# Retention attention feeding a GELU MLP: a hand-ordered two-stream schedule with groups of 256 to 768 tokens and loads by chunk

## Chip, cores, metric

One core of a Trainium2 chip. The time is the device time of one execution in microseconds (us), the median of several. Executions of one kernel agree within about 1% here, apart from one of the kernel before at 354.67 us, which is left out. Engines: PE is TensorE, DVE VectorE, ACT ScalarE, Pool GpSimd. Lines such as L66 are source lines of the kernel at hand.

## The reference, cut

```python
# q, k, v: [4 batches, 8 heads, 768 tokens, 64]; lam: [8]; w_in: [512, 2048]; w_out: [2048, 512]
intra = (qb @ kb.T * Dmask) @ vb                 # Dmask[i, j] = lam ** (i - j) for i >= j
inter = (qb * lam ** (pos + 1)) @ kv_state       # the state runs over the blocks of a sequence
kv_state = lam ** block * kv_state + (kb * lam ** (block - 1 - pos)).T @ vb
x = attention, [3072 tokens, 512]
out = gelu(x @ w_in) @ w_out                     # exact gelu
```

Both kernels work in bf16 with chunks of 128 tokens, 24 in all, 6 to a batch. They scale rows by lam^pos and lam^-pos, so that the mask is plainly triangular.

## The kernel before

The parts that matter (cuts marked). Its tool orders the instructions; the source order is only the dataflow.

```python
TOK = 256
def attn_batch(b, psum):
    # one load per tensor and batch, [128, H, NB, D]
    nc.gpsimd.dma_start(q_t, q[b].rearrange("h (so si) d -> si h so d", si=128))    # k_t, v_t alike
    for sb in range(NB):                                                  # 6 chunks
        nc.gpsimd.tensor_mul(q_hat, q_t[:, :, sb, :], lam_pos_b)
        nc.gpsimd.tensor_mul(k_hat, k_t[:, :, sb, :], lam_neg_b)
        # ... 8 transposes on PE, two copies on DVE, 8 score matmuls on PE
        nc.vector.tensor_mul(sc_m, sc_ps, cmask_b)
        # ... 16 output matmuls, a copy to xT_sb on ACT; 8 matmuls k_hat.T v,
        # ... two state additions and one state multiplication on DVE
def moe_chunk(t, psum_m, psum_mo):
    for kf in range(NK2):                                                 # 16 feature blocks
        # ... 4 matmuls of N=256 into h_ps (two buffers)
        nc.scalar.activation(gT, h_ps, ACT.Gelu)
        for io in range(NO):                                              # 2 token tiles
            nc.tensor.matmul(om[io], gT[:, io * 128:(io + 1) * 128], w_out_t[:, kf, :], ...)   # N=512
for b in range(B):
    attn_batch(b, psum)
    # ... after batch 0: one load each of w_in and w_out
    for t in range(b * (S // TOK), (b + 1) * (S // TOK)):
        moe_chunk(t, moe_psum, moe_out_psum)
```

## Time and profile before

| | before |
|---|---|
| median of the three fast runs | 297.76 us (297.51 to 298.76; 298.26 with the slow one) |
| profiled span | 296.9 us |
| PE busy, with overlapping latencies | 238.1 us |
| DVE, ACT, Pool busy | 85.6, 103.8, 94.7 us |
| MLP's own matmuls at their warm spacing | 167 us |

### The profile page before, as it was taken

The page shows a single profiled execution, that of the slowest core. Times are in us where ns is not written, and L with a number is a line of the kernel's source. Part 1 is how long each engine was busy: PE and PEld are TensorE (multiplying, and loading weights), DVE is VectorE, ACT ScalarE, POOL GpSimd, SP SyncE. Part 2 cuts the span into 40 slices and gives each one's busy share as a digit, 9 for nine tenths or more (in the row PEclk, how much of TensorE's full clock was granted, in tenths as well). Part 3 has the DMA queues.
Part 4 walks back from the last instruction along what each step waited for, and adds up shares of the span by engine and source line. Part 5 has one row for each costly group of instructions (what it writes and reads, how often), then busy time and mean ns, then how long its engine had stood idle before and what let it go on. Part 6 is the DMA issues. An engine that isn't in the chain of part 4 may idle for free.

```text
span 296.9 us, 5123 instructions
## 1 busy us (share of the span) xinstructions
PE 238.1 (80%) x2081; PEld 145.1 (49%) x2112; DVE 85.6 (29%) x150; ACT 103.8 (35%) x247; POOL 94.7 (32%) x119
## 2 busy tenths in 40 slices
PE   0037295999999789999999799999998789999893
PEld 0025162555555456655554555555555556555451
DVE  1037544400000679500000768300003778100000
ACT  4001221343344323353534223453533133453532
POOL 7474625847200778610000645300003531000000
PEclk9999997999999969999999879999999689999999
DMA  6996999999990194990010100010101000010101
GB/s 44 157 118 116 187 192 126 123 146 137 154 174 0 71 80 30 106 152 27 6 68 0 73 0 2 2 71 0 73 1 56 17 2 1 2 71 2 71 1 71
DMA packets 80135, 20.25 MB, mean 68 GB/s; under 512 B 74480, under 2 KB 76528, under 8 KB 80112
## 3 DMA queue, kind: packets, MB, share of 16 engines
q0 software_dynamic: 76512, 13.63, 67.0%
q1 hardware_dynamic: 3600, 6.30, 5.6%
q8 instruction: 16, 0.26, 0.4%
q14 instruction: 7, 0.06, 0.1%
HBM read 27.27 MB, written 6.29 MB: 113 GB/s over the span
## 4 chain that ended last, share of the span: by engine, by line
PE 60%; ACT 12%; DMA 9%; issue 7%; DVE 6%; POOL 4%; ACTq 1%; POOLq 0%
PE omps L167 32%; PE h_ps L162 16%; ACT gT L165 11%; DMA w_out_t<-in_moe_w_out_dram 5%; DMA k_t<-in_k_dram 4%; PE sc_ps L124 3%; PE out_ps L135 3%; DVE sc_m L130 3%; PE out_ps L136 2%; PE kT_ps L113 2%; POOL q_hat L104 1%; DVE kv_state_new L153 1%; PE qT_ps L112 1%; POOL k_hat L105 1%; PE kv_ps L143 1%
## 5 line engine op out<-in xcount | busy, mean ns | idle before, releaser
L162 PE MATMUL h_ps<-xT_sb,w_in_t 128*128 128x256 bf16 x768 | 116.4, 279 | 4.0 <-DMA w_in_t<-in_moe_w_in_dram 4.0
L167 PE MATMUL omps<-w_out_t,gT 128*128 128x512 bf16 x353 | 105.3, 386 | 15.8 <-ACT gT L165 4.4
L165 ACT ACTIVATE gT<-h_ps 128x256 bf16<-128x256 f32 x192 | 73.1, 384 | 127.2 <-PE h_ps L162 117.2
L162 PEld LDWEIGHTS <-w_in_t 128*128 128x128 bf16 x768 | 76.0, 100 | 42.1 <-DMA w_in_t<-in_moe_w_in_dram 4.3
L167 PEld LDWEIGHTS <-gT 128*128 128x128 bf16 x384 | 29.6, 98 | 50.6 <-ACT gT L165 35.9
L104 POOL TENSOR_TENSOR q_hat<-q_t,lam_pos 128x512 bf16<-128x512 bf16 x24 | 25.1, 1052 | 78.3 <-PE qT_ps L112 57.7
L116 DVE COPY qT<-qT_ps 128x512 bf16<-128x512 bf16 x24 | 10.1, 421 | 122.5 <-PE qT_ps L112 119.8
L130 DVE TENSOR_TENSOR sc_m<-sc_ps,cmask 128x1024 bf16<-128x1024 f32 x24 | 29.4, 1224 | 28.8 <-PE sc_ps L124 28.7
L105 POOL TENSOR_TENSOR k_hat<-k_t,lam_neg 128x512 bf16<-128x512 bf16 x24 | 25.7, 1071 | 34.5 <-PE kv_ps L143 26.9
L138 ACT CAST xT_sb<-out_ps 128x512 bf16<-128x512 f32 x24 | 14.0, 585 | 55.4 <-PE out_ps L136 55.4
L112 PE MATMUL qT_ps<-ident,q_hat 128*128 128x128 bf16 x96 | 12.3, 251 | 17.2 <-POOL q_hat L104 17.1
L135 PE MATMUL out_ps<-sc_m,v_t 128*64 128x128 bf16 x192 | 16.5, 248 | 7.2 <-DVE sc_m L130 6.0
L153 DVE TENSOR_TENSOR kv_state_new<-kv_state_new,lam_blk 128x512 bf16<-128x512 bf16 x24 | 18.0, 749 | 1.8
L112 PEld LDWEIGHTS <-q_hat 128*128 128x128 bf16 x96 | 7.9, 111 | 19.8 <-POOL q_hat L104 17.6
L124 PE MATMUL sc_ps<-qT,kT 64*128 64x128 bf16 x192 | 11.4, 247 | 5.7 <-DVE kT L117 5.4
L149 POOL MEMSET kv_state_new<- 64x256 bf16 x24 | 7.3, 306 | 27.0 <-PE out_ps L136 26.3
L135 PEld LDWEIGHTS <-v_t 128*64 128x64 bf16 x192 | 12.9, 125 | 5.7 <-issue 5.3
L113 PE MATMUL kT_ps<-ident,k_hat 128*128 128x128 bf16 x96 | 11.8, 245 | 3.6 <-POOL k_hat L105 2.5
L171 ACT COPY out_sb<-omps 128x512 f32<-128x512 f32 x24 | 12.9, 589 | 4.8 <-PE omps L167 4.6
L136 PE MATMUL out_ps<-qT,kv_state_new 128*64 128x128 bf16 x160 | 13.6, 245 | 0.0
L117 DVE COPY kT<-kT_ps 128x512 bf16<-128x512 bf16 x24 | 10.1, 420 | 11.0 <-PE kT_ps L113 10.6
L96 POOL DMA_DIRECT2D v_t<-in_v_dram x4 | 8.9, 2225 | 12.8 <-DMA q_t<-in_q_dram 6.0
(35 smaller groups left out, 100.1 us busy)
## 6 DMA issues: line engine op xcount, KB each, us to landing
out_dram<-out_sb SPq DMA_DIRECT2D x24, 256.0 KB, 2.2
q_t<-in_q_dram POOLq DMA_DIRECT2D x4, 768.0 KB, 9.5
k_t<-in_k_dram POOLq DMA_DIRECT2D x4, 768.0 KB, 11.6
v_t<-in_v_dram POOLq DMA_DIRECT2D x4, 768.0 KB, 10.8
w_in_t<-in_moe_w_in_dram POOLq DMA_DIRECT2D x1, 2048.0 KB, 13.5
w_out_t<-in_moe_w_out_dram POOLq DMA_DIRECT2D x1, 2048.0 KB, 15.1
lam_b<-in_lam_dram SPq DMA_DIRECT2D x1, 4.0 KB, 2.5
```

The source lines that it names most:

```text
L104: nc.gpsimd.tensor_mul(q_hat, q_t[:, :, sb, :], lam_pos_b)
L105: nc.gpsimd.tensor_mul(k_hat, k_t[:, :, sb, :], lam_neg_b)
L112: nc.tensor.transpose(qT_ps[:, hp * C:(hp + 1) * C], q_hat[:, 2 * hp:2 * hp + 2, :], ident)
L113: nc.tensor.transpose(kT_ps[:, hp * C:(hp + 1) * C], k_hat[:, 2 * hp:2 * hp + 2, :], ident)
L124: nc.tensor.matmul(sc_ps[:, (hi * HP + hp) * C:(hi * HP + hp + 1) * C], kT[hi * D:(hi + 1) * D, hp * C:(hp + 1) * C], qT[hi * D:(hi + 1) * ...
L130: nc.vector.tensor_mul(sc_m, sc_ps.rearrange("p (h c) -> p h c", h=H), cmask_b)
L135: nc.tensor.matmul(osl, vb[:, h, :], sc_m[:, hi * HP + hp, :], start=True, stop=False)
L136: nc.tensor.matmul(osl, kv_state[:, h * D:(h + 1) * D], qT[:, hp * C:(hp + 1) * C], start=False, stop=True)
L153: nc.vector.tensor_mul(kv_state_new, kv_state_new, lam_blk_hd)
L162: nc.tensor.matmul(h_ps, w_in_t[:, ki, kf * 128:(kf + 1) * 128], x_t[:, ki, :], start=(ki == 0), stop=(ki == NK1 - 1))
L165: nc.scalar.activation(gT, h_ps, ACT.Gelu)
L167: nc.tensor.matmul(om[io], gT[:, io * 128:(io + 1) * 128], w_out_t[:, kf, :], start=(kf == 0), stop=(kf == NK2 - 1))
```

## The change

Its intent is to keep PE on MLP matmuls and to slip the pieces of the next group's attention between them at fixed places, so that neither the gelu nor the attention's chain is waited for. The diff is 409 lines; this is its core.

```diff
-    TOK = 256
+    groups = [6, 2, 4, 4, 4, 4]                 # chunks of 128 tokens in a group
+    ctx.enter_context(tc.manual_schedule())     # every engine runs in source order
+    def load_piece(b, name, lo, hi):            # one load per tensor and chunk, [128, NB, H, D]
+        for so in range(lo, hi):
+            nc.gpsimd.dma_start(qkv[b, name][:, so, :, :],
+                src[b, :, so * C:(so + 1) * C, :].rearrange("h si d -> si h d"))
+    # batch 0: chunks 0 and 1, constants, chunks 2 to 5, then w_in and w_out in 4 slices each
+    def hats(n):                                # Pool; k is no longer scaled, v is
+        nc.gpsimd.tensor_mul(c.q_hat, ..., lam_pos_b)
+        nc.gpsimd.tensor_mul(c.v_hat, ..., lam_neg_b)
+    # transposes: one copy of q and k on DVE; scores: mask and state additions on DVE,
+    # state multiplication on Pool; outputs: state product as 4 full 128x128 matmuls, copy on DVE
+    # mlp_blocks: first all of mm1 (4 matmuls, gelu), then mm2 (4 matmuls a block)
+    live[0] = hats(0)                           # lead-in: group 0 alone
+    for n in range(groups[0]):
+        transposes(live[n])
+        if n + 1 < groups[0]: live[n + 1] = hats(n + 1)
+        scores(live[n]); outputs(live[n], xT[0], n)
+    load_batch(1)                               # 18 loads
+    for g in range(len(groups)):
+        first = 0.45 if g == 0 else 0.0
+        at = lambda f: (first + (0.97 - first) * (i + f) / m) * total
+        def step(kind):
+            if kind == 0:
+                if n % NB == 0 and n // NB + 1 < B: load_batch(n // NB + 1)
+                live[n] = hats(n)
+            # ... 1 transposes, 2 scores, 3 outputs
+        todo += [(at(-0.3), 0, step), (at(0.05), 1, step), (at(0.4), 2, step), (at(0.75), 3, step)]
+        # ... MLP blocks in order, each step issued once its place is reached
```

## The prediction

> **What bounds the kernel now.** I read first the page's busy times and slices, then the windows by stage, then the steady part of the timeline, then the Pool engine's own timeline at the start.
>
> ```profile
> span 296.9 us, 5123 instructions
> PE 238.1 (80%) x2081; PEld 145.1 (49%) x2112; DVE 85.6 (29%) x150; ACT 103.8 (35%) x247; POOL 94.7 (32%) x119
> PEclk9999997999999969999999879999999689999999
> ```
>
> PE (TensorE) carries the time; nothing else is above 35%. But 238.1 us counts overlapping matmul latencies, so it is no measure of what PE needs. The third line is the clock by slice: after the first batch it dips three more times, at the starts of batches 1 to 3.
>
> The windows of three stages: MLP alone, the start of batch 1, the start.
>
> ```profile
> core 0: us, PE busy (x) PEld busy (x) DVE busy (x) ACT busy (x) POOL busy (x), PEclk, DMA share, GB/s
> 0.00:37.00 37.00, 9.65 (x112) 6.43 (x112) 12.72 (x24) 6.05 (x9) 22.19 (x30) 1.00 1.73 124
> ...
> 98.00:107.00 9.00, 6.17 (x92) 4.38 (x90) 7.67 (x15) 2.24 (x4) 7.87 (x8) 0.77 0.16 60
> ...
> 190.00:228.00 38.00, 35.50 (x230) 20.81 (x232) 0.61 (x2) 16.48 (x42) 0.56 (x1) 1.00 0.08 29
> ```
>
> So there are three losses. At the start PE has little to do for 37 us. At a batch start (98 to 107) the attention chain of 128-token chunks runs nearly alone, with DVE busy 7.67 of 9 us and PE's clock at 0.77. And inside the MLP PE waits for the gelu. That last one is in the timeline of the steady part:
>
> ```profile
> 87.03 0.82 ACT L165 ACTIVATE gT<-h_ps 128x256 bf16<-128x256 f32 x2 [1.19 <-PE h_ps L162]
> 87.47 0.11 PEld L167 LDWEIGHTS <-gT 128*128 128x128 bf16 x2 [0.38 <-ACT gT L165]
> ...
> 89.05 0.82 ACT L165 ACTIVATE gT<-h_ps 128x256 bf16<-128x256 f32 x2 [1.19 <-PE h_ps L162]
> 89.48 0.11 PEld L167 LDWEIGHTS <-gT 128*128 128x128 bf16 x2 [0.38 <-ACT gT L165]
> ```
>
> Two feature blocks repeat every 2.01 us. From the same view, seven N=256 matmuls take 0.93 us with 0.27 of latency, so they start (0.93 - 0.27)/6 = 0.11 us apart; four N=512 ones take 1.04 with 0.38, so 0.22 apart. The work of two blocks is 8 x 0.109 + 4 x 0.217 = 1.74 us. So 0.27 us in 2.01, 13%, is waiting. Over 96 such pairs that is 26 us.
>
> PE's floor is then: MLP 768 x 0.109 + 384 x 0.217 = 167 us, plus attention. The remaining 100 us are what a better order could save.
>
> Pool at the start is the view on which my prediction turns:
>
> ```profile
> 1.82 2.39 POOL L94 DMA_DIRECT2D q_t<-in_q_dram  x1
> 4.21 2.22 POOL L95 DMA_DIRECT2D k_t<-in_k_dram  x1
> 11.85 2.22 POOL L96 DMA_DIRECT2D v_t<-in_v_dram  x1 [5.42 <-DMA q_t<-in_q_dram]
> 14.08 1.05 POOL L104 TENSOR_TENSOR q_hat<-q_t,lam_pos 128x512 bf16<-128x512 bf16 x1
> ...
> 23.54 0.81 POOL L180 DMA_DIRECT2D w_in_t<-in_moe_w_in_dram  x1
> ...
> 33.42 1.22 POOL L181 DMA_DIRECT2D w_out_t<-in_moe_w_out_dram  x1
> ```
>
> A load occupies Pool while it is issued, and the multiplication behind it starts only then (14.08 follows 11.85 + 2.22). By the source, a batch load moves 6144 rows of 64 numbers, w_in 512 long rows, w_out 2048. A line through 0.81, 1.22 and about 2.25 us is 0.68 us plus 0.26 us per 1000 rows.
>
> **The Trainium skill.** "TensorE: Matmul & The Clock Gate", Wait — 56ns, not 53.3ns?, gives a warm spacing of N/2.4 GHz plus 2.5 ns: 109 and 216 ns at N = 256 and 512. The trace agrees. The same page, What's actually happening, says that the clock halves after about 3.4 us of idle and returns after as much work; the dips agree, and in the first chunks the trace shows the N=128 transposes at twice their later spacing. "DMA: Bandwidth & Descriptors", Anatomy of one DMA, calls descriptor generation small and says many come before the cost shows up; here it is 0.81 to 2.39 us of Pool per load, and the measurement decides. "Perfetto Trace Analysis", DMA Instruction — SWDGE (GPSIMD), says the reported end of such an instruction is the end of descriptor generation; the trace agrees, as Pool's next work begins there.
>
> **The change part by part.**
>
> *Loads by chunk.* 12 loads become 72 of 1024 rows. Each costs 0.68 + 0.27 = 0.95 us of Pool (estimate from the line above); a batch goes from 6.7 to 17.1 us of Pool. Eight weight slices of 512 rows cost 0.81 each, 6.5 us. Data lands as fast as before (a tensor of a batch about every 5.2 us), so the landing is no limit. But the new order is fixed: all 18 loads of batch 0 and all 8 weight slices stand in front of the first multiplication. Pool is free at about 0.8 + 17.1 + 1.1 (constants) + 6.5 = 25.5 us. The first multiplication was at 14.08 before.
>
> *Six attention chunks alone.* DVE per chunk, scaled from the rows of the page (0.42 for 512 bf16 out of PSUM, 1.22 for 1024 f32, 0.42 for 256 f32, so 0.155 us plus elements at 1 or 2 per 0.96 GHz cycle): one joint copy of q and k transposed 0.69, mask 1.22, two state additions 0.84, and the copy of the result, moved from ACT, 0.69; 3.44 in all. The wait for the scores between copy and mask is 0.65, handoffs 0.2. That is 4.3 us a chunk, and Pool's 3.2 (two multiplications of 1.05, two half-size ones estimated at 0.55) fits below. First transposes at 26.5, copy at 27.5, six chunks: the MLP starts at about 53 us. The weights have landed by then (some 27 us after about 20).
>
> *512-token groups.* The first matmuls are N=384, 256 and 512. Sum of the MLP: 128 x 0.163 + 64 x 0.109 + 256 x 0.216 + 384 x 0.216 = 166 us, as before. The second matmuls now come after all 16 gelus, so the wait of 0.27 per pair goes. What remains is the double-buffered PSUM tile: four matmuls, 0.1 us, then the gelu (0.384 us at 256; about 0.59 at 512, as the equal-sized ACT copies take 0.585). A pair of N=512 blocks needs 1.78 us against 1.73 of work, N=384 1.47 against 1.30, N=256 1.14 against 0.87: 16 x 0.05/2 x 4 + 32 x 0.085 + 16 x 0.13, so 6 us, of which I keep 5 since attention pieces fill some.
>
> *Attention between the matmuls.* From warm stretches of the timeline: transposes 0.44, scores 0.33, state product 0.25, outputs about 0.22 + 0.3. That is 1.5 us per chunk, 27 us for 18, now without the chain's waits or cold clock.
>
> *Loads ahead of use.* The load of a batch is issued just ahead of the first multiplication of the batch before it. Batches 1 and 2 go out back to back after the lead-in: Pool is free at about 49.5, and 34 us later, at 83.6, multiplies chunk 6. PE meets chunk 6's transposes at fraction 0.463 of the first group, at 53 + 1.7 (cold) + 30 blocks x 0.735, some 77 us. It waits about 7.5 us. Batch 3 is loaded after chunk 11's multiplication, some 3 us before group 1 ends, 17 us of Pool, plus 1 us for the multiplication, while PE wants chunk 12 one block into group 2. It waits about 14.5 us. Each wait exceeds 3.4 us, so some 1.7 us more at half clock.
>
> Sum: start 53, MLP 166, attention 27, gelu 5, cold start 2, Pool waits 22, cold after them 3.5, short handoffs 3, and the end as now 4.5 (last matmul 292.4 to 296.9). 286 us.
>
> **The rivals.** (a) *Pool is not in the way.* If the issue of small loads overlaps more than I reckon (0.5 us each), the start shortens by 8, the first wait goes and the second halves: about 262. For it: a hand-tuned order should not have been left with such waits, and the fraction 0.45 for the first group looks tuned. Against it: three row counts lie on one line, and the fixed 0.68 is paid for each. (b) *The order on PE binds.* PE is in order, so pieces that come too early stall it. In group 1 four chunks share 14 us of MLP: 1.2 us of matmuls lie between scores and outputs, and mask and latencies take 1.6. If every chunk lost 1 us so, 18 us would come on top: about 300. Against it: in the four-chunk groups 2 to 4 there are 2.4 us between pieces. (c) *Vector becomes the bound.* 24 x 3.4 = 82 us in 286; no. (d) *The long lead-in gives back all of the gain*, as it is 4 us longer than the 49 us at which the MLP gets going now. It can't undo it: the waits of 26 us and the three batch starts are gone whatever the start costs.
>
> **Range and chances.** The sum is 286. My largest term is Pool's 0.95 us: 0.1 us less gives 7 us. The likelier error is that I overrate Pool's waits, so I put the time a little under the sum, at 282, and the range at 264 to 294. Below 291.8 counts as faster by over 2%: 0.83; within 2% 0.14; slower 0.03.
>
> **What would show it.** Right: Pool at work on loads without a break up to about 25 us and the first transposes just after; 4.3 us per chunk in the lead-in; the first gelu at 53 to 55; two PE waits for a multiplication on Pool, of some 7 and 14 us, each with the clock down after it; between them N=512 matmuls every 0.216 us. Wrong: first transposes before 20 us, or no such waits (then 255 to 265), or many waits of PE for the mask in each group (then about 300).

## More of the kernel before

The span is far longer than what the matmuls need back to back; the question is which waits make up the rest. The prediction shows the lines of the page, the windows and the timelines for that. One more, the chain of waits that ended last, by engine:

```profile
PE 60%; ACT 12%; DMA 9%; issue 7%; DVE 6%; POOL 4%; ACTq 1%; POOLq 0%
```

Pool is 4% of that chain.

## The result

The changed kernel took 285.61 us (284.87 to 287.21, four runs). The ratio of fast runs is 0.959, 95% interval 0.955 to 0.964. Ratios are the mean time of one kernel's fast runs over that of the other's of the same rounds, so not quite the ratio of the medians quoted. It is 4% faster; the range held, and the sum of 286 us was nearer than the 282 put down.

The page of the changed kernel, its head, its clock by slice and its chain by engine:

```profile
span 284.4 us, 3912 instructions
...
PE 223.2 (78%) x1648; PEld 117.3 (41%) x1648; DVE 78.4 (28%) x116; ACT 78.9 (28%) x143; POOL 140.7 (49%) x169
...
PEclk9999999999968999999958999999999999999999
...
PE 62%; POOL 29%; DVE 4%; issue 4%; ACT 0%; POOLq 0%; ACTq 0%; DVEq 0%
```

Pool has gone from 94.7 to 140.7 us of work, but above all from 4% to 29% of the chain. ACT and the DMA are off it. Two clock dips are left in the clock line, each where PE has stood still. (That line shows nothing of the lead-in, although its four transposes take 0.58 to 0.61 us each time, against 0.39 to 0.40 later.) The waits are in PE's timeline (start, length, line, what, and in brackets how long PE was idle and what ended it):

```profile
25.62 0.61 PE L147 MATMUL t_ps<-ident,q_hat 128*128 128x128 bf16 x4 [25.62 <-POOL q_hat L140]
...
52.98 22.38 PE L208 MATMUL h_ps<-x_t,w_in_t 128*128 128x384 bf16 x120
82.44 0.61 PE L147 MATMUL t_ps<-ident,q_hat 128*128 128x128 bf16 x4 [7.08 <-POOL q_hat L140]
...
117.15 0.40 PE L147 MATMUL t_ps<-ident,q_hat 128*128 128x128 bf16 x4 [0.85 <-POOL q_hat L140]
123.23 0.40 PE L147 MATMUL t_ps<-ident,q_hat 128*128 128x128 bf16 x4 [0.85 <-POOL q_hat L140]
130.16 0.40 PE L147 MATMUL t_ps<-ident,q_hat 128*128 128x128 bf16 x4 [1.50 <-POOL q_hat L140]
148.00 0.61 PE L147 MATMUL t_ps<-ident,q_hat 128*128 128x128 bf16 x4 [11.60 <-POOL q_hat L140]
```

All six waits are for a multiplication on Pool. Pool's timeline says what stood before it:

```profile
16.71 0.96 POOL L66 DMA_DIRECT2D k_t<-in_k_dram  x1
17.58 0.97 POOL L66 DMA_DIRECT2D v_t<-in_v_dram  x1
18.45 3.08 POOL L123 DMA_DIRECT2D w_in_t<-in_moe_w_in_dram  x4
21.39 3.10 POOL L126 DMA_DIRECT2D w_out_t<-in_moe_w_out_dram  x4
24.49 1.07 POOL L140 TENSOR_TENSOR q_hat<-q_t,lam_pos 128x512 bf16<-128x512 bf16 x1
...
131.05 0.94 POOL L66 DMA_DIRECT2D q_t<-in_q_dram  x1
...
145.85 1.02 POOL L66 DMA_DIRECT2D v_t<-in_v_dram  x1
146.75 1.20 POOL L140 TENSOR_TENSOR q_hat<-q_t,lam_pos 128x512 bf16<-128x512 bf16 x1
```

Pool issues loads, with a few short constants between the first of them, up to 24.49 us, and again from 131.05 to 146.75, 15.7 us for the 18 loads of batch 3. From start to start a load takes 0.87 us, although it is listed with up to 1.02.

### The profile page after: what moved, and what is told of

Read it like the earlier page. It is cut to its first block, busy times and chain, and to the rows that moved or that the text cites. A ratio compares the mean times of both kernels' runs of the same rounds, so it can differ in the third digit from the quotient of the medians.

```text
span 284.4 us, 3912 instructions
## 1 busy us (share of the span) xinstructions
PE 223.2 (78%) x1648; PEld 117.3 (41%) x1648; DVE 78.4 (28%) x116; ACT 78.9 (28%) x143; POOL 140.7 (49%) x169
## 4 chain that ended last, share of the span: by engine, by line
PE 62%; POOL 29%; DVE 4%; issue 4%; ACT 0%; POOLq 0%; ACTq 0%; DVEq 0%
PE o_ps L220 28%; PE h_ps L208 22%; POOL q_t L66 7%; POOL k_t L66 7%; POOL v_t L66 7%; PE sc_ps L158 3%; PE t_ps L147 3%; PE t_ps L149 2%; POOL q_hat L140 2%; POOL state L181 2%; PE o_ps L191 2%; DVE state L177 1%; DVE qkT L151 1%; POOL w_in_t L123 1%; POOL w_out_t L126 1%
## 5 line engine op out<-in xcount | busy, mean ns | idle before, releaser
L208 PE MATMUL h_ps<-x_t,w_in_t 128*128 128x512 bf16 (+2 forms) x448 | 94.2, 360 | 0.1
L210 ACT ACTIVATE g_t<-h_ps 128x512 bf16<-128x512 f32 (+2 forms) x112 | 60.1, 536 | 110.7 <-PE h_ps L208 110.3
L220 PE MATMUL o_ps<-w_out_t,g_t 128*128 128x512 bf16 x384 | 88.7, 381 | 0.0
L181 POOL TENSOR_TENSOR state<-state,lam_blk 64x256 bf16<-64x256 bf16 x32 | 21.4, 669 | 100.9 <-DVE state L177 99.5
L208 PEld LDWEIGHTS <-w_in_t 128*128 128x128 bf16 x448 | 43.2, 100 | 40.7 <-issue 7.3
L220 PEld LDWEIGHTS <-g_t 128*128 128x128 bf16 x384 | 35.7, 98 | 40.4 <-issue 1.1
L151 DVE COPY qkT<-t_ps 128x1024 bf16<-128x1024 bf16 x24 | 16.6, 692 | 102.1 <-PE t_ps L149 102.1
L141 POOL TENSOR_TENSOR v_hat<-v_t,lam_neg 128x512 bf16<-128x512 bf16 x24 | 25.3, 1055 | 0.0
L66 POOL DMA_DIRECT2D q_t<-in_q_dram x24 | 22.9, 954 | 0.8 <-POOLq L303 0.8
L66 POOL DMA_DIRECT2D k_t<-in_k_dram x24 | 22.5, 939 | 0.0
```

The costliest lines, as they stand in the source:

```text
L66: nc.gpsimd.dma_start(qkv[b, name][:, so, :, :], src[b, :, so * C:(so + 1) * C, :].rearrange("h si d -> si h d"))
L141: nc.gpsimd.tensor_mul(c.v_hat, qkv[c.b, "v"][:, c.sb, :, :], lam_neg_b)
L151: nc.vector.tensor_copy(c.qkT, t_ps)
L181: nc.gpsimd.tensor_mul(new[p, :, p], new[p, :, p], lam_blk_r[p, :, hi, :])
L208: nc.tensor.matmul(h_ps, w_in_t[:, ki, kf * 128:(kf + 1) * 128], x_t[:, ki, sub * N:(sub + 1) * N], start=(ki == 0), stop=(ki == NK1 - 1))
L210: nc.scalar.activation(g_t[:, kf, sub * N:(sub + 1) * N], h_ps, ACT.Gelu)
```

## The experiments

Ten more kernels, each right in its result, timed in three rounds beside the kernel before (medians 298.0 to 298.6 us).

### Are the two long waits due to whole batches of loads on Pool?

**e1_spread**: the same 72 loads, spread.

```diff
-    load_batch(1)
+    for n in range(groups[0], groups[0] + 4): load_chunk(n)     # 3 loads
...
-                        if n % NB == 0 and n // NB + 1 < B: load_batch(n // NB + 1)
                         live[n] = hats(n)
+                        if n + 4 < NCH: load_chunk(n + 4)
```

> Same 72 loads, same Pool time in all, but spread: chunks 6 to 9 are loaded after the lead-in, then each multiplication of chunk n is followed by the loads of chunk n+4. Theory (Pool's issue of whole batches stands in front of the multiplications): PE's waits of 7.08 and 11.60 us before the transposes of chunks 6 and 12 vanish, with some 1.5 us of half clock after each; 285.6 - 18.7 - 3 = 264 us. Rival (the waits are for the data, or PE's fixed order has other waits close behind): waits of about the same size stay or come back elsewhere, 278 to 286 us.

264.03 us, ratio 0.884 (0.881 to 0.886). In PE's timeline the first group now runs through:

```profile
69.69 6.70 PE L208 MATMUL h_ps<-x_t,w_in_t 128*128 128x384 bf16 x38
76.23 0.39 PE L147 MATMUL t_ps<-ident,q_hat 128*128 128x128 bf16 x4
76.45 0.39 PE L149 MATMUL t_ps<-ident,k_t 128*128 128x128 bf16 x4
76.67 1.46 PE L208 MATMUL h_ps<-x_t,w_in_t 128*128 128x384 bf16 x8
```

The transposes of chunk 6 come with no wait, and the one of 11.60 us is gone too; three short ones in group 1 stay (0.86, 0.98, 1.51 us). Pool's busy time is unchanged (141.1 us). So it wasn't the amount of Pool's work but its place: 21.6 us, more than the change had gained as a whole.

**e4_halves**: every load of batches 1 to 3 in two of 512 rows, same rows and bytes.

```diff
+                for hh in range(2):
+                    hs = slice(hh * H // 2, (hh + 1) * H // 2)
-                load_piece(b, name, so, so + 1)
+                    nc.gpsimd.dma_start(qkv[b, name][:, so, hs, :], src[b, hs, ...])
```

> Each load of batches 1 to 3 is split in two of 512 rows; rows and bytes stay. Theory: a batch takes 36 x 0.81 = 29 us of Pool instead of 16.3, so the first wait grows by 2 x 12.9 to about 33 us and the second by 12.9 to about 24.5; 285.6 + 38.7 = 324 us. Rival (waits for data): unchanged within 2 us.

319.17 us, ratio 1.069: the waits before chunks 6 and 12 are 28.09 and 22.51 us.

```profile
104.18 0.61 PE L147 MATMUL t_ps<-ident,q_hat 128*128 128x128 bf16 x4 [28.09 <-POOL q_hat L140]
180.79 0.61 PE L147 MATMUL t_ps<-ident,q_hat 128*128 128x128 bf16 x4 [22.51 <-POOL q_hat L140]
```

The dose works as expected and is a little smaller, since a half load starts 0.73 us after the last one rather than 0.81. The rival, that PE waits for data, expected no change.

**e3_one_load**: fewer loads. In batches 1 to 3 q and v are one load each. k can't be: it is transposed unscaled, so the two heads of a transpose must lie side by side, which the layout of a single load doesn't give.

```diff
-        for so in range(NB):
-            for name in "qkv": load_piece(b, name, so, so + 1)
+        for name, src in (("q", q), ("v", v)):              # [128, H, NB, D]
+            nc.gpsimd.dma_start(qkv[b, name], src[b].rearrange("h (so si) d -> si h so d", si=C))
+        load_piece(b, "k", 0, NB)
```

> In batches 1 to 3 q and v are one load each again (k has to stay by chunk, since it is transposed unscaled and its two heads must lie side by side). Rows and bytes are the same, loads 42 fewer with 30 ... per batch 8 instead of 18. Theory (a fixed 0.68 us of Pool per load): a batch takes 2 x 2.25 + 6 x 0.9 = 9.9 us of Pool instead of 16.3; the first wait (7.08) goes, the second falls from 11.6 to about 5.2; 285.6 - 7.1 - 6.4 - 2 = 270 us. Rival (Pool's time is by rows, or the data is awaited): unchanged, 284 to 287 us.

(The garbled clause means: 8 loads a batch instead of 18.) 281.54 us, not 270; the waits are 4.58 and 8.98 us. The theory missed. Pool's timeline shows why:

```profile
49.84 2.29 POOL L240 DMA_DIRECT2D q_t<-in_q_dram  x1
52.12 2.23 POOL L240 DMA_DIRECT2D v_t<-in_v_dram  x1
54.33 2.65 POOL L66 DMA_DIRECT2D k_t<-in_k_dram  x3
59.97 2.63 POOL L66 DMA_DIRECT2D k_t<-in_k_dram  x3 [3.00 <-issue]
66.38 2.21 POOL L240 DMA_DIRECT2D q_t<-in_q_dram  x1 [3.78 <-issue]
69.14 2.22 POOL L240 DMA_DIRECT2D v_t<-in_v_dram  x1 [0.55 <-issue]
71.35 2.64 POOL L66 DMA_DIRECT2D k_t<-in_k_dram  x3
76.51 2.63 POOL L66 DMA_DIRECT2D k_t<-in_k_dram  x3 [2.52 <-issue]
79.21 1.04 POOL L140 TENSOR_TENSOR q_hat<-q_t,lam_pos 128x512 bf16<-128x512 bf16 x1
```

The issue work is as short as expected (2.29 + 2.23 + 2 x 2.64 = 9.8 us a batch), but Pool now stands still between loads. Two batches still took 29.3 us, 14.7 each, near the 15.6 us in which three tensors land at 5.2 us each. The view names only "issue" for the gaps, but by the landing times in the trace each ends 0.31 to 0.35 us after an earlier load has landed (q_t of batch 1 at 59.64, v_t at 66.07). So the loads wait for landings, as v_t's did in the kernel before. Here it is not for a semaphore (a counter by which a load tells that it has landed): the program's loads take eight in turn, and those of the held loads had been free for 3 us or more. All five gaps of the run fit one limit, an estimate from these landings: a load waits if it would bring the rows in flight to 16,384 or more, while 15,360 were let through. No run tested that limit. Issue and landing of a batch are thus about equally long, and shortening one runs into the other. Placing the loads elsewhere, as in e1, gets round both; issuing them from an engine other than Pool was not tried.

### Does an earlier start count?

**e2_early**: multiplications of chunks 0 and 1 first, the other loads between the lead-in's chunks, each weight in one load; batches 1 to 3 as in the change.

```diff
-    # chunks 2 to 5 and 8 weight slices ahead of everything
     live[0] = hats(0)
+    live[1] = hats(1)
+    load_so(2); load_so(3)
     for n in range(groups[0]):
         transposes(live[n])
+        if n in (2, 3): load_so(n + 2)
+        if n == 4: nc.gpsimd.dma_start(w_out_t, w_out_r)
         # ... hats(n + 1)
+        if n == 1: nc.gpsimd.dma_start(w_in_t, w_in_r)
```

> The multiplications of chunks 0 and 1 come before the other loads of batch 0, those are issued between the lead-in's chunks, each weight is one load. Theory (the first PE work waits for Pool's 26 loads, not for data): first transposes at about 9 us instead of 25.6, but Pool then needs about 6.2 us for a chunk with loads in it, so the MLP starts at about 41.5 us instead of 53.0; both later waits stay at 7 and 11.6; 285.6 - 11.5 = 274 us. Rival (the start is bound by the landing of batch 0 and of w_in): MLP not before 50 us, 282 to 286 us.

285.25 us: nothing gained, as the rival had it, but not for its reason. PE's timeline:

```profile
45.21 23.34 PE L194 MATMUL h_ps<-x_t,w_in_t 128*128 128x384 bf16 x120
81.92 0.61 PE L133 MATMUL t_ps<-ident,q_hat 128*128 128x128 bf16 x4 [13.37 <-POOL q_hat L126]
```

The MLP does start 7.8 us earlier (3.7 short of what I expected; Pool waited 3.79 us for chunk 4's q, whose load stood behind w_in's transfer). But chunk 6's transposes come at 81.92, against 82.44 before, and the wait has grown from 7.08 to 13.37. Pool's timeline has the cause:

```profile
48.42 0.93 POOL L66 DMA_DIRECT2D q_t<-in_q_dram  x1
54.15 0.88 POOL L66 DMA_DIRECT2D k_t<-in_k_dram  x1 [4.79 <-DMA w_out_t<-in_moe_w_out_dram]
```

A load of batch 1 was held until w_out, issued eight loads before, had landed. Here it is the eight semaphores: each load waits for the landing of the one eight before it. From there on eight stayed in flight, and they started every 0.92 us instead of 0.87. So the 36 loads began 6.5 us earlier than in the changed kernel (43.16 against 49.65), and the last of them started at nearly the same time (79.88 against 80.35). So the start is worth something only if what comes next isn't bound to the same point.

**e5_early_spread**: both together, chunks 4 and 5 ahead of w_in.

```diff
+    LEAD = {1: [4, 5, 'w_in'], 3: ['w_out'], 5: [6, 7, 8]}      # issued after the scores of chunk n
+    AFTER = {6: [9, 10], 7: [11], ..., 19: [23]}                # issued after the multiplications of n
```

> e1's spread loads and e2's early multiplications together, with w_in and w_out one load each, placed so that no load stands ahead of w_in that isn't needed before it. Theory (e2 gained nothing because the time won at the start was lost again in the wait for whole batches behind w_out): with spread loads the start counts in full. MLP from about 41.5 us instead of 53, no wait over 2 us after it: 264 - 11.5 = 252.5 us. Rival (the loads' data is the bound at the start, 42 us of transfers for batch 0 and the weights): MLP not before 48 us, or new waits for data of 8 us or more: 259 to 264 us.

252.46 us, ratio 0.845. The MLP starts at 41.72 us, and the early start now counts in full: 264.03 - 252.46 = 11.6 us, where e2 had shown none of its 7.8.

**e6_groups_of_4**: the same with six groups of four chunks.

```diff
-    groups = [6, 2, 4, 4, 4, 4]          -    first = 0.45
+    groups = [4] * 6                     +    first = 0.3
+    pre = (2, 3, 'w_in0', 'w_in1');  LEAD = {2: [4], 3: [5, 'w_out0']}
+    AFTER = {4: ['w_out1', 6], 5: [7], 6: [8, 9], 7: [10], ...}
```

> As e5, with six groups of four chunks (only four chunks alone, no N=384 or 256) and the weights in halves, the second half of w_out behind the first group's start. Theory: MLP from about 29 us; 166 for the MLP, 20 chunks at 1.69 us, 2 cold, 3 for gelu and handoffs, 4 at the end: 238, at most 243 us. Rival (data of w_in, w_out and chunks 6 and 7 isn't there in time): waits for DMA of 5 us or more in the first group, 245 to 252 us.

238.35 us, ratio 0.798 (0.797 to 0.800). Its page:

```profile
span 236.0 us, 3747 instructions
...
PE   0355699999999999999999999999999999999993
```

The MLP starts at 29.80, and PE is at 90% or more in every slice from the sixth to the last but one. No wait for Pool is left after the lead-in. This beats both kernels: 20% below the one before, 17% below the changed one by the medians.

### What did the parts of the change bring?

**e7_two_phase**: the kernel before, with only this taken over:

```diff
-    TOK = 256
+    TOK = 384
         for kf in range(NK2):
             # ... 4 matmuls
-            nc.scalar.activation(gT, h_ps, ACT.Gelu)
-            for io in range(NO): nc.tensor.matmul(om[io], ...)
+            nc.scalar.activation(gT[:, kf, :], h_ps, ACT.Gelu)
+        for io in range(NO):
+            for kf in range(NK2): nc.tensor.matmul(om, gT[:, kf, ...], ...)
```

> The kernel before, with one thing of the change alone: groups of 384 tokens whose second matmuls come after all 16 gelus. Attention, loads and the tool's own order stay as before. Theory (of the gain, the part inside the MLP is a wait for the gelu in every pair, 26 us, of which a double buffer of N=384 keeps 128 x 0.045 = 6): about 298.5 - 20 = 278 us. Rival (that wait was filled with attention anyway, or the new order puts other waits in its place): 290 us or more.

277.80 us, ratio 0.931 (0.927 to 0.935). The wait for the gelu is worth about the 20 us. The trace agrees: the MLP starts at 37.2 us, as before (37.1), and its gelus repeat in pairs every 1.39 us (134.67 and 136.06) for 1.30 us of work. The larger groups and the new order came together here and were not tried apart. This part alone is better than the whole change (285.61), so the rest of the change, as it stands, cost about 8 us net.

**e8_serial**: e1 with the interleaving undone.

```diff
-                at = lambda f: (first + (0.97 - first) * (i + f) / m) * total
+                at = lambda f, i=i: total + i + f
```

> e1 with the interleaving undone: the attention of the next group comes after the present group's MLP. Theory (interleaving takes a chunk from 4.56 us alone, as in the lead-in, to 1.69): 18 x 2.87 = 52 us more, less 3 us of handoffs, plus some 1.7 us of half clock after each of five stretches: 264 + 57 = 321 us, over 20 us slower than the kernel before. Rival (the chain of a chunk is mostly PE work, or the tool's order did as well): below 295 us.

340.79 us, 20 more than expected. A chunk alone took 6.68 us, not the 4.56 of the lead-in. I put that down to the loads that follow each multiplication and moved them.

**e9_serial_b**: the loads for a group ahead of the MLP before it.

```diff
+            for n in range(starts[g + 1], starts[g + 1] + m):
+                if n + AHEAD < NCH: load_chunk(n + AHEAD)
...
-                        if n + AHEAD < NCH: load_chunk(n + AHEAD)
```

> e8 without what confounded it: there the three loads behind each multiplication lay in the chain from one chunk to the next (6.68 us a chunk instead of 4.56). Here the loads for a group are issued ahead of the MLP that precedes it. Theory (a chunk alone takes 4.6 us, between matmuls 1.69): as expected of e8, 264 + 57 = 321 us. Rival (e8's 341 was due to the serial order itself): 335 us or more.

340.48 us: that explanation was wrong. Pool's timeline, now without loads in the chain:

```profile
127.63 1.41 POOL L181 TENSOR_TENSOR state<-state,lam_blk 64x256 bf16<-64x256 bf16 x2 [7.77 <-DVE state L177]
129.11 1.04 POOL L140 TENSOR_TENSOR q_hat<-q_t,lam_pos 128x512 bf16<-128x512 bf16 x1
130.11 1.04 POOL L141 TENSOR_TENSOR v_hat<-v_t,lam_neg 128x512 bf16<-128x512 bf16 x1
134.31 1.41 POOL L181 TENSOR_TENSOR state<-state,lam_blk 64x256 bf16<-64x256 bf16 x2 [3.15 <-DVE state L177]
135.79 1.04 POOL L140 TENSOR_TENSOR q_hat<-q_t,lam_pos 128x512 bf16<-128x512 bf16 x1
```

The next chunk's multiplication, whose data has long been there, stands behind the present chunk's state multiplication, which waits for DVE. Pool is idle for 3.15 us just ahead of that state multiplication. In the lead-in the source has them the other way round.

**e10_serial_c**: only that order changed.

```diff
-                todo += [(at(-0.3), 0, step), ...]
+                todo += [(at(-0.65), 0, step), ...]
```

> e9 with one number changed: the multiplication of chunk n+1 is issued before the scores of chunk n, as in the lead-in, so on Pool it no longer stands behind chunk n's state multiplication (1.41 us), which waits for DVE. Theory (this order, not the loads, made 6.68 us of 4.56): the ten waits of PE for q_hat, 21.4 us after the start, go: 340.5 - 21.4 = 319 us, which is then the price of the serial order alone. Rival (something else in the serial order): 332 us or more.

320.82 us, as expected of e8 at first. PE waits for q_hat only once, at the start. So the serial order costs 57 us against e1, and interleaving is worth about that much once the loads are out of the way. (e10 also has e9's places for the loads; from e8 to e9 these made 0.3 us.) The three short waits in group 1 of the changed kernel (0.85, 0.85, 1.50 us) have the form of e9's: before 117.15, 123.23 and 130.16 us Pool did the state multiplication and then q_hat. Removing them alone was not tried.

## Why the prediction was right

Its sum, term by term, against the trace of the changed kernel (the MLP's term is worked out from spacing again, not measured as a sum; the last but one is what remains):

| term | predicted us | measured us |
|---|---|---|
| first MLP matmul | 53 | 52.98 |
| MLP matmuls | 166 | 166 |
| 18 chunks between them | 27 | 18 x 1.69 = 30.4 |
| the two waits for Pool | 7.5 + 14.5 | 7.08 + 11.60 |
| short handoffs | 3 | 3.2 |
| gelu, cold clock | 5 + 2 + 3.5 | 9 |
| end | 4.5 | 4.1 |
| sum | 286 | 284.4 |

The sum came out closer than its terms: the chunks were put 3.4 us too low and the waits 3.3 us too high.

**Pool at the start** held: loads without a break to 24.49 us, the first transposes at 25.62. That the lead-in's chunk takes 4.56 us and not 4.3 cancels against Pool being free a microsecond sooner.

**The two waits** were predicted with their places, and e1 and e4 show their cause by taking it away and by enlarging it. The first came out by some luck: Pool was done 2.3 us sooner than predicted (81.35 against 83.6) and PE arrived 1.6 us sooner (75.36 against 77). The second was 2.9 us too long in the prediction. Half of that is that 18 loads take 15.7 us and not 17.1: a load overlaps the next by about 0.1 us, which the line through single loads couldn't show. The rest is that the loads started 5.35 us before PE wanted chunk 12 (131.05 and 136.40), not some 3.6.

**The short handoffs** agree by luck. The 3.2 us measured are the three waits for Pool in group 1, which the prediction did not name.

**Landing is no limit**, I wrote. It is no limit of the changed kernel, but only just: from 60.14 us on seven earlier loads are in flight at each new one, of the eight that the semaphores allow, and e3 ran into a limit of landings at once.

**The gelu term** was too large. Pairs of N=384 blocks take 1.39 us in the trace (the gelu repeats at 63.64 and 65.03), not 1.47, and those of N=512 have no such wait at all: in the last group 64 first matmuls run every 0.216 us. A chunk's pieces took 1.69 us instead of 1.5: the outputs, with the four matmuls on the state, take 0.67 of PE, not 0.52.

**The clock.** Half speed after the two long waits came as predicted: four transposes take 0.61 us at 82.44 and 148.00. But the prediction's reading that the dips of the kernel before agree with 3.4 us of idle is wrong. At the start of batch 1 the granted clock goes to half at 102.88 us in the trace, the eight score matmuls go from 0.40 to 0.61 us, and no idle time of PE since 98 us was over 0.81 us:

```profile
99.19 0.40 PE L124 MATMUL sc_ps<-qT,kT 64*128 64x128 bf16 x8
...
100.91 0.25 PE L135 MATMUL out_ps<-sc_m,v_t 128*64 128x128 bf16 x2 [0.75 <-DVE sc_m L130]
...
103.32 0.61 PE L124 MATMUL sc_ps<-qT,kT 64*128 64x128 bf16 x8 [0.81 <-DVE kT L117]
```

In e10 the same happens at 129.71 us, after no wait over 0.79 us. There the measurement decides: half speed came with only short waits before it. How busy PE must be to keep its speed, no run here settles.

**The rivals.** (a), Pool not in the way, fell with e1 and e4. (b), PE's order: group 1 does have waits, 3.2 us in all, but by the timeline for Pool's order, and not for the mask. (c), DVE: 78.4 us of work in 284. (d), the lead-in eating the gain: the wait inside the MLP was worth 20 us (e7), the bunched loads gave 21.6 back (e1), and the start another 11.6 (e1 to e5). The gain was given back to Pool's queue, not missed on PE.

**The one poor choice** was the step from the sum of 286 to 282, for the reason that a hand-tuned order should have no such waits. The profile gave no ground for that, and the sum was better alone.

## What to carry to other kernels

An engine that both issues loads and computes is a queue: whatever stands in front is waited for, even if the data of what follows is there. So put loads behind the work that is due sooner and spread them by use, rather than making them fewer. When an order is fixed by hand, walk each engine's queue, not only PE's: here a busy share of 49% hid 29% of the chain. A gain at one place is worth nothing until the next thing bound to the old time is moved as well (e2 against e5).

## What the Trainium skill lacked or had wrong

- "DMA: Bandwidth & Descriptors", Anatomy of one DMA, calls descriptor generation small, variable, and slow to show. Here 18 loads of 1024 rows hold Pool for 15.7 us, 0.87 us each from start to start; single loads of 512, 2048 and 6144 rows take 0.81, 1.22 and 2.2 to 2.4 us.
- The same page doesn't tell that a load on Pool can itself wait for earlier loads: in e3 idle times of 3.00 and 3.78 us end 0.33 and 0.32 us after a landing. (The waits of 5.42 us in the kernel before and 4.79 us in e2 are for a semaphore, and so the program's own.) The gaps in e3 fit a limit just under 16,384 rows in flight; no run tested it.
- "TensorE: Matmul & The Clock Gate", Back-to-back issue gap, gives a sustained 81 ns at N = 128 and 131 ns at N = 512 for pairs of weight load and matmul. The traces show 216 ns at N = 512, and eight transposes of N = 128 in 0.44 us, 55 ns each, between MLP matmuls. The formula of that section fits; the sustained figures don't.
- That Pool's queue is worked in order is in the skill, but no page that I read says what this can cost: one multiplication behind a waiting one cost 19.7 us over the kernel (e9 against e10).
